# A Strassen–Winograd feed-forward kernel: two groups' second-matrix tiles kept for the first unit, its operands begun one group sooner, transposes moved to other gaps, and weight sums reordered

## The chip, the cores and the metric

The kernel runs on one core of one Trainium2 chip. The metric is the device time of one execution in microseconds (us). The tensor engine (PE) ran at a granted clock of 1.00 of full speed in every stretch looked at, so no difference here is one of clock.

## What is computed

The reference chains three blocks over a batch of 2 and a sequence of 768:

```python
x = attention(q, k, v)        # 8 heads of 64; a band of 31 keys beside block maxima of keys, block means of values
u = x + (relu(xt @ w_tok1) @ w_tok2).T          # over the sequence
x = u + relu(u @ w_ch1) @ w_ch2                 # 512 -> 1536 -> 512
xn = (x - mean) / sqrt(var + 1e-6) * g_ln
out = x + relu(xn @ w_ch1b) @ w_ch2b            # 512 -> 2048 -> 512
```

Float32 results are made of pairs of reduced-precision numbers, a high and a low part, so each product is three matmuls (high by high, high by low, low by high; lines L316, L317, L318).

## The kernel before, in words

Attention and the token mixing fill the first 95 us. From about 95 to 308 us stands the 512 to 1536 block, a loop over groups `(s, f, g)`: `g3` makes one first product (`g_('u', g)_f`, 12 matmuls 128x384) in a PSUM bank of the pool `ps_mm`; ScalarE (ACT, L700) makes the high part `ah` of its relu and VectorE (DVE, L701) the low part `al`; `g4` then makes three tiles of the second product (`acc`, three matmuls 128x512 each). Tiles of one group run between the first products of the next ones.

From 308 us on stands the last block as sixteen *units*. Units 0 to 7 (`unit`, for half the sequence) and 8 to 15 (`unit1`, the other half) each make seven Strassen–Winograd products `m`, of six matmuls 128x384. What a product leaves in its bank is taken up by adds into the running sums: `sm` by a copy of product 0 on ACT (L848), then `um`, `sm`, `wm`, `sm`, `wm` and `um`, `um` on DVE (L836), for products 1 to 6. Two of them read product 5. Behind the adds the relu parts are made (L827 on ACT, L828 on DVE). Between the products stand tiles `acc_x` of the unit before, which wait in the queue `pending`: `flow` issues ceil(pending / products left) of them behind product k, and then calls `step(k)`. In a unit of 2 to 7 twelve tiles wait, two behind each of the first five products, one behind each of the last two.

Three things are woven into that:

- **Transposes.** `prep_x(s)` makes the operands of the Strassen products from the normalized activations: eight times ACT normalizes (L623), PE transposes (`tx`, L656, three 128x128), ACT copies it out with a scale (L660), and ACT and DVE split it into parts (L641, L642) and sum operands (L671 to L683). `prep_x(0)`, for units 0 to 7, runs in the last groups of the block before. `prep_x(1)`, for units 8 to 15, starts in unit 1 and has two transposes in each of units 2 to 5.
- **Weight sums.** `w2_sums(p)`, p = 0 to 7, makes combinations of the second matrix for units 8 to 15: two adds `wx` (L787), three into `wt` (L796 to L799), two casts `wk` on ACT (L805), two subtractions on DVE (L809), two stores (L810, `w2t<-wk`, on SP's queue). For p of 2 and more, `wx` reads the second matrix of unit p where the unit itself reads it: two slots hold it, loaded in halves (L763, `slot<-w2s`). For p = 0 and 1 the matrix is read a second time (`read_again`, L773). The `wk` tiles live in the pool `spill`, with two buffers, so a cast waits until the store of two tiles earlier has landed.
- **Weight decoding** (`convert_all`), which ends in unit 1.

`ps_mm` has two banks, and products and transposes share them. So what comes behind a transpose needs the bank of the product ahead of the transpose, and waits until its adds have read it. On PE the order is the one in which the code issues (`manual_schedule`). On the other engines a scheduler orders the instructions by their readiness and priority; once built, the order is fixed, and an instruction that waits holds up those behind it on its engine. All loads and stores of this stretch are issued by SP.

Of the kernel before, what the change touches and what calls it, by code (L numbers as in the profile page):

```python
# [15 lines left out]
ALU = mybir.AluOpType  # L16
# [23 lines left out]
NP = F2 // 2  # L40
# [25 lines left out]
def f32(ap):  # L66
    return ap.bitcast(F32)


class Kern:  # L70
# [705 lines left out]
    def w2_sums(self, p):  # L776
        nc = self.nc
        tt = nc.vector.tensor_tensor
        new = lambda k: self.long(f"{k}{p}")
        if p < 2:  # L780
            src = self.again.pop(p)
        else:
            w = f32(self.w2_at(p))
            src = [w[:, 512 * i : 512 * i + 512] for i in range(4)]
        x = new("wx")
        for f in range(2):
            tt(x[:, 512 * f : 512 * f + 512], src[2 * f], src[2 * f + 1], op=ALU.add)  # L787
            if f:
                self.read.add(p)
                if p == 0:  # L790
                    self.read_again(1)
            yield
        t = new("wt")
        b = x.rearrange("p (f j n) -> p f j n", f=2, j=2)
        k = t.rearrange("p (k n) -> p k n", k=4)
        tt(k[:, 0:2], b[:, :, 1], b[:, 0], op=ALU.subtract)  # L796
        yield
        tt(k[:, 2], k[:, 0], b[:, 1, 1], op=ALU.subtract)
        tt(k[:, 3], k[:, 2], b[:, 1, 0], op=ALU.add)  # L799
        yield  # L800
        out = []
        for e in range(2):
            w = self.spill.tile([P, 1024], F32R, tag="sp", name=f"wk{e}_{p}")
            v = self.blocks(w)
            nc.scalar.copy(v[:, :, 0], k[:, 2 * e : 2 * e + 2])  # L805
            out.append((w, v))
        yield
        for e, (w, v) in enumerate(out):
            tt(v[:, :, 1], k[:, 2 * e : 2 * e + 2], f32(v[:, :, 0]), op=ALU.subtract)  # L809
            nc.sync.dma_start(self.w2t[p][:, 2 * e : 2 * e + 2].rearrange("p k t n -> p (k t n)"), f32(w))  # L810
            if e == 0:
                yield
        self.summed.add(p)
        yield
# [16 lines left out]
    def unit(self, n, pending, step):  # L831

        nc = self.nc
        s, p = divmod(n, NP)
        new = lambda k: self.tmp.tile([P, GN], F32, tag=k, bufs=1, name=f"{k}m_{n}")
        add = lambda o, x, y: nc.vector.tensor_tensor(o, x, y, op=ALU.add)  # L836
        bank = lambda k: self.ps_mm.tile([P, 512], F32, tag="mm", name=f"m{k}_{n}")
        a = {}
        for k in range(7):
            q = bank(k)  # L840
            self.product(7 * n + k, s, k, q)
            self.load_w1(7 * n + k + RING)
            q = q[:, :GN]
            urgent = ExitStack()
            urgent.enter_context(self.tc.high_priority(URGENT))
            if k == 0:
                s1 = new("s")
                nc.scalar.copy(s1, q)  # L848
            elif k == 1:
                u = new("u")  # L850
                add(u, q, s1)
            elif k == 2:
                add(s1, q, s1)
                a["C11"] = self.relu(f"{n}_11", s1)
            elif k == 3:
                w = new("w")
                add(w, q, u)
            elif k == 4:
                c = new("s")
                add(c, q, w)  # L860
                a["C12"] = self.relu(f"{n}_12", c)
            elif k == 5:
                add(w, q, w)
                a["C22"] = self.relu(f"{n}_22", w)
                add(u, q, u)
            else:
                add(u, q, u)
                a["C21"] = self.relu(f"{n}_21", u)
            urgent.close()
            self.flow(n, k, pending, step)  # L870
        self.load_w2(n + 1)
        out = []
        for name in ("C11", "C12", "C22", "C21"):
            f, i = int(name[1]) - 1, int(name[2]) - 1
            for j in range(GT):
                out.append((name, j, lambda f=f, i=i, j=j, x=a[name]: self.second(n, f, i, j, x)))
        return deque(x[2] for x in out)
# [256 lines left out]
    def run(self):  # L1134
        tc, nc, ctx = self.tc, self.nc, self.ctx
# [56 lines left out]
        first = self.small.tile([P, 1], F32, tag="first", name="first")  # L1192
# [16 lines left out]
        y = self.g2(1)  # L1209
        self.bg += [None] + [y] * ST  # L1210
        units = []
# [13 lines left out]
        later, pending = deque(), deque()  # L1225
        for n, (s, f, g) in enumerate(units):
# [10 lines left out]
                self.bg += [self.transpose_u(g + 2)] * CC  # L1237
            if f == 2 and s == 1:
                self.bg += [self.norm_stats(g - 2)] * (GT + 1)
            if (s, f, g) == (1, 5, 3):  # L1240
                later += [self.prep_x(0)] * 9
            elif later:
                self.bg.append(later.popleft())
            if prev is not None:
                while 2 * prev[1] + 1 not in self.half:
                    self.convert_all(4)
                blocks = self.g4(*prev)
                if n == len(units) - 1:
                    pending += blocks
                else:  # L1250
                    for fn in blocks:
                        fn()
                if prev[0] == ("u", 3) and prev[1] == 11:
                    for k in range(9):
                        self.load_w1(k)
                    self.load_w2(0)
# [29 lines left out]
        order.enter_context(tc.manual_schedule(engines={E.PE}))  # L1286
        pending += self.g4(*prev)
        self.summed, self.read, self.kp, self.again = set(), set(), {}, {}
        sums = (x for p in (2, 3, 4, 5, 0, 6, 1, 7) for x in self.w2_sums(p))
        pending.popleft()()  # L1290
        for n in range(2 * NP):

            def step(k):
                if n == 0 and k == 6:
                    for r in range(9, RING):
                        self.load_w1(r)
                self.convert_all(((2, 2, 2, 2, 2, 1, 0) if n == 0 else (3, 2, 2, 3, 2, 0, 2))[k])
                if (n, k) == (4, 0):
                    self.read_again(0)
                if n == 1 or n in range(2, 6) and k in (1, 5):  # L1300
                    for _ in range(2 if n == 1 and k in (1, 4) else 1):
                        self.start(1)
                        self.finish()

                if n > 2 or n == 2 and k > 5:
                    for _ in range((2, 0, 1, 2, 2, 0, 2)[k] if n < 6 else 2 if n == 7 or k in (0, 4) else 1):
                        next(sums, None)

            if n == 1:
                self.bg += [self.norm_stats(2)] * (GT + 1) + [self.norm_stats(3)] * (GT + 1)  # L1310
                self.bg += [self.prep_x(1)] * 9
            pending = (self.unit1 if n >= NP else self.unit)(n, pending, step)
# [89 lines left out]
```

## Time and profile before

| | us |
|---|---|
| device time, median of 3 runs (lowest, highest) | 569.76 (568.62, 571.74) |
| the profiled execution: its own time | 570.52 |
| the profiled execution: first to last instruction (span) | 568.5 |
| PE busy | 557.3 (98%) |
| VectorE busy | 404.7 (71%) |
| ScalarE busy | 274.8 (48%) |

The profile is of one execution, with times counted from its first instruction. A matmul's row gives its start, and an end that is modelled: the next matmul starts well before it. So a stall on PE is read from the distance between two starts, against the usual distance. A row of the timeline has start, duration, engine, line, operation, and what it writes and reads. A bracket gives the idle time of the engine ahead of it, and what ended that.

### The profile page before, as it was taken

The page shows a single profiled execution, that of the slowest core. Times are in us where ns is not written, and L with a number is a line of the kernel's source. Part 1 is how long each engine was busy: PE and PEld are TensorE (multiplying, and loading weights), DVE is VectorE, ACT ScalarE, POOL GpSimd, SP SyncE. Part 2 cuts the span into 40 slices and gives each one's busy share as a digit, 9 for nine tenths or more (in the row PEclk, how much of TensorE's full clock was granted, in tenths as well). Part 3 has the DMA queues.
Part 4 walks back from the last instruction along what each step waited for, and adds up shares of the span by engine and source line. Part 5 has one row for each costly group of instructions (what it writes and reads, how often), then busy time and mean ns, then how long its engine had stood idle before and what let it go on. Part 6 is the DMA issues. An engine that isn't in the chain of part 4 may idle for free.

```text
span 568.5 us, 10249 instructions
## 1 busy us (share of the span) xinstructions
PE 557.3 (98%) x3685; PEld 496.1 (87%) x3685; DVE 404.7 (71%) x977; ACT 274.8 (48%) x608; POOL 18.7 (3%) x41
## 2 busy tenths in 40 slices
PE   9999999999999999999999999999999999999997
PEld 4777779899998889889888898888898999999997
DVE  4998773647867887655568975768886876677771
ACT  4997673237755554544787234354333223333320
POOL 0011620000000000000000000000000000000000
PEclk9999999999999999999999999999999999999999
DMA  9969810425788878879757996787888998777545
GB/s 284 324 196 297 266 72 1 148 92 188 241 282 286 293 266 280 310 265 324 246 186 224 300 319 180 239 261 232 285 293 266 325 309 267 233 230 236 172 147 187
DMA packets 63655, 135.75 MB, mean 239 GB/s; under 512 B 5747, under 2 KB 22899, under 8 KB 63606
## 3 DMA queue, kind: packets, MB, share of 16 engines
q1 hardware_dynamic: 63600, 135.09, 72.1%
q8 instruction: 29, 0.48, 0.4%
q14 instruction: 20, 0.16, 0.1%
q10 hardware_dynamic: 6, 0.02, 0.0%
HBM read 100.49 MB, written 34.60 MB: 238 GB/s over the span
## 4 chain that ended last, share of the span: by engine, by line
PE 76%; DVE 7%; DMA 7%; ACT 6%; issue 2%; POOL 1%; ACTq 0%; POOLq 0%; DVEq 0%
PE m L316 7%; PE m L318 6%; PE m L317 6%; PE acc_x L318 3%; PE acc_x L317 3%; PE acc_x L316 3%; DMA slot<-w2s 2%; PE acc_y L318 2%; PE g L533 2%; PE acc_y L317 2%; PE acc_y L316 2%; ACT pr L477 2%; DMA w1s<-sps 1%; PE warm_ps L1132 1%; DMA stage<-in_wts_dram 1%
## 5 line engine op out<-in xcount | busy, mean ns | idle before, releaser
L316 PE MATMUL m<-slot,slot 128*128 128x384 f32 (+1 forms) x141 | 47.5, 337 | 1.1 <-DVE um L836 0.9
L318 PE MATMUL m<-slot,slot 128*128 128x384 f32 (+1 forms) x141 | 46.9, 332 | 0.0
L317 PE MATMUL m<-slot,slot 128*128 128x384 f32 (+1 forms) x141 | 46.8, 332 | 0.0
L318 PE MATMUL acc_x<-slot,al 128*128 128x512 f32 x96 | 37.8, 394 | 0.0
L317 PE MATMUL acc_x<-slot,ah 128*128 128x512 f32 x96 | 37.8, 394 | 0.0
L316 PE MATMUL acc_x<-slot,ah 128*128 128x512 f32 x96 | 37.5, 391 | 0.0
L477 ACT ACTIVATE pr<-sn,mn 128x120 f32<-128x120 f32 x96 | 29.9, 386 | 4.8 <-DVE mn L462 4.7
L316 PEld LDWEIGHTS m<-slot,slot 128*128 128x128 f32 x141 | 26.5, 188 | 4.2 <-DVE um L836 1.9
L317 PEld LDWEIGHTS m<-slot,slot 128*128 128x128 f32 x141 | 26.5, 188 | 1.6
L318 PEld LDWEIGHTS m<-slot,slot 128*128 128x128 f32 x141 | 26.5, 188 | 0.0
L827 ACT ACTIVATE ah<-sm 128x384 fp32r<-128x384 f32 x16 | 8.4, 524 | 36.7 <-DVE sm L836 36.7
L141 ACT ACTIVATE dec<-stage 128x512 f32<-128x512 f32 x36 | 24.4, 677 | 2.4 <-DMA stage<-in_wts_dram 2.4
L164 DVE SCALAR_TENSOR_TENSOR dec<-stage,dec 128x512 uint32<-128x512 uint32 x36 | 24.8, 688 | 0.9
L462 DVE CUSTOM_DVE_ANT_0 sn<-scores,mask 128x120 f32<-128x120 f32 x96 | 21.2, 277 | 5.4 <-PE scores L443 5.3
L533 PE MATMUL g<-u,tok 128*128 128x256 f32 x96 | 21.6, 381 | 0.0
L318 PEld LDWEIGHTS acc_x<-slot,al 128*128 128x128 f32 x96 | 18.0, 188 | 4.0
L168 DVE SCALAR_TENSOR_TENSOR dec<-stage,dec 128x512 uint32<-128x512 uint32 x23 | 15.9, 690 | 7.3 <-ACT stage L141 7.3
L318 PE MATMUL acc_y<-slot,al_s 128*128 128x256 f32 x72 | 20.1, 280 | 0.0
L533 PEld LDWEIGHTS g<-u,tok 128*128 128x128 f32 x96 | 17.9, 190 | 2.5 <-issue 0.2
L317 PE MATMUL acc_y<-slot,ah_s 128*128 128x256 f32 x72 | 20.1, 279 | 0.0
L623 ACT ACTIVATE xn<-u,nb,rs 128x128 f32<-128x128 f32 x48 | 20.1, 484 | 0.0
L316 PE MATMUL acc_y<-slot,ah_s 128*128 128x256 f32 x72 | 20.0, 278 | 0.0
(1493 smaller groups left out, 1707.1 us busy)
## 6 DMA issues: line engine op xcount, KB each, us to landing
stage<-in_wts_dram SPq DMA_DIRECT2D x62, 512.0 KB, 4.5
slot<-w1s SPq DMA_DIRECT2D x94, 256.0 KB, 3.7
w1s<-sps SPq DMA_DIRECT2D x16, 512.0 KB, 3.6
w2s<-sp SPq DMA_DIRECT2D x16, 512.0 KB, 3.9
slot<-w2s SPq DMA_DIRECT2D x16, 512.0 KB, 5.0
w2t<-wk SPq DMA_DIRECT2D x16, 512.0 KB, 4.6
slot<-w2t SPq DMA_DIRECT2D x8, 768.0 KB, 5.0
slot<-w2s SPq DMA_DIRECT2D x22, 256.0 KB, 4.4
```

The lines of the kernel that those rows point to most:

```text
L141: fold = lambda out: nc.scalar.activation(out, high, AF.Prelu, scale=2.0**-112, alpha=-(2.0**32))
L164: put(m, t[:, :, 0], 29, m, op0=ALU.logical_shift_right, op1=ALU.bitwise_or)
L168: put(m, t[:, :, 1], 3, m, op0=ALU.logical_shift_left, op1=ALU.bitwise_or)
L316: nc.tensor.matmul(out, lhs[0], rhs[0], start=first, stop=False)
L317: nc.tensor.matmul(out, lhs[0], rhs[1], start=False, stop=False)
L318: nc.tensor.matmul(out, lhs[1], rhs[0], start=False, stop=last)
L462: nc.vector.tensor_tensor_reduce(sn[:, u], ps[:, u % 2, u // 2, :NK], self.mask[:, mv], scale=-SCALE, scalar=3e38, op0=ALU.add, op1=ALU.mi ...
L477: self.nc.scalar.activation(self.pr[n][:, u], sn[:, u], AF.Exp, bias=mn[:, u : u + 1], scale=-1.0)
L533: nc.tensor.matmul(ps[:, :256], self.tok1(st, t), self.u[:, b * ST + st, 256 * hf : 256 * hf + 256], start=st == 0, stop=st == ST - 1,)
L623: nc.scalar.activation(xn[:, j], self.u[:, g * GT + j, cc * P : cc * P + P], AF.Identity, bias=nb[:, j : j + 1], scale=rs[:, j : j + 1],)
L827: nc.scalar.activation(ah, x, AF.Relu)
L1132: self.nc.tensor.matmul(self.wps, self.warm[:, :P], self.warm, start=True, stop=True)
```

## The change

The change has four parts. The tiles `acc` of the last two groups of the 512 to 1536 block join `pending`, not those of the last alone; two of them are issued ahead of unit 0, not one. `prep_x(0)` is put into the loop at group (1, 8, 2), not (1, 5, 3). The transposes of `prep_x(1)` in units 2 to 5 stand behind products 1 and 3 (counted from 0), not 1 and 5. The weight sums of p = 2 to 7 and those of p = 0 and 1 run as two sequences, with new places in the units, `read_again(0)` moves from unit 4 to unit 2, and each `wx` add is issued behind the add `um`, `sm` or `wm` that the code issued last.

```diff
@@ w2_sums
         for f in range(2):
-            tt(x[:, 512 * f : 512 * f + 512], src[2 * f], src[2 * f + 1], op=ALU.add)
+            with self.tc.issue_after(self.reader.ins):
+                tt(x[:, 512 * f : 512 * f + 512], src[2 * f], src[2 * f + 1], op=ALU.add)
@@ unit
-        add = lambda o, x, y: nc.vector.tensor_tensor(o, x, y, op=ALU.add)
+        def add(o, x, y):
+            self.reader = nc.vector.tensor_tensor(o, x, y, op=ALU.add)
+
@@ run
-            if (s, f, g) == (1, 5, 3):
+            if (s, f, g) == (1, 8, 2):
                 later += [self.prep_x(0)] * 9
...
-                if n == len(units) - 1:
+                if n >= len(units) - 2:
                     pending += blocks
...
-        sums = (x for p in (2, 3, 4, 5, 0, 6, 1, 7) for x in self.w2_sums(p))
-        pending.popleft()()
+        sums = (x for p in range(2, NP) for x in self.w2_sums(p))
+        first = (x for p in range(2) for x in self.w2_sums(p))
+        for _ in range(2):
+            pending.popleft()()
...
-                if (n, k) == (4, 0):
+                if (n, k) == (2, 0):
                     self.read_again(0)
-                if n == 1 or n in range(2, 6) and k in (1, 5):
+                if n == 1 or n in range(2, 6) and k in (1, 3):
...
-                if n > 2 or n == 2 and k > 5:
-                    for _ in range((2, 0, 1, 2, 2, 0, 2)[k] if n < 6 else 2 if n == 7 or k in (0, 4) else 1):
+                if n > 1:
+                    for _ in range((0, 0, 1, 1, 2, 1, 2)[k]):
                         next(sums, None)
+                if 2 < n < 7 and k < 2:
+                    for _ in range(1 if (n, k) in ((3, 0), (5, 1)) else 2):
+                        next(first, None)
```

On PE the first transpose of `prep_x(0)` moves ahead of the product `g_('u', 3)_9`. The difference there (+ is a row of the changed kernel):

```order
 L316 MATMUL acc_('u', 3)_0_2841<-slot_1544,ah_('u', 3)_8_3211 128x512
 L317 MATMUL acc_('u', 3)_0_2841<-slot_1544,ah_('u', 3)_8_3211 128x512
 L318 MATMUL acc_('u', 3)_0_2841<-slot_1544,al_('u', 3)_8_3212 128x512
+L656 MATMUL tx_0_3263<-ident,xn_0_3218 128x128 x3
 L316 MATMUL acc_('u', 3)_1_2842<-slot_1544,ah_('u', 3)_8_3211 128x512
 L317 MATMUL acc_('u', 3)_1_2842<-slot_1544,ah_('u', 3)_8_3211 128x512
```

So `g_('u', 3)_9`, which comes six matmuls later, has a transpose between itself and the product `g_('u', 2)_12`, where before it had none.

On PE at the end of unit 0, before (`m5_0` is product 5 of unit 0, `m0_1` product 0 of unit 1; the rows between repeat these):

```order
L318 MATMUL m5_0_3760<-slot6_1542,slot8_1544 128x384
L316 MATMUL m6_0_3774<-slot9_1545 128x384
...
L318 MATMUL m6_0_3774<-slot9_1545 128x384
L316 MATMUL m0_1_3792<-slot3_104,extra_1744 128x384
L317 MATMUL m0_1_3792<-slot3_104,extra_1744 128x384
```

and in the changed kernel:

```order
L318 MATMUL m5_0_3752<-slot6_1542,slot8_1544 128x384
L316 MATMUL acc_('u', 3)_1_2842<-slot2_103,ah_('u', 3)_14_3625 128x512
...
L316 MATMUL m6_0_3770<-slot9_1545 128x384
...
L316 MATMUL acc_('u', 3)_2_2843<-slot2_103,ah_('u', 3)_14_3625 128x512
...
L316 MATMUL m0_1_3792<-slot3_104,extra_1744 128x384
```

Three products stood back to back, and now a tile of three matmuls stands between each two.

On DVE in unit 2 and the start of unit 3, before (`wm_2<-m3_2` is the add that reads product 3 of unit 2, `wx3` the weight sum of unit 3's matrix in `slot11`):

```order
L836 TENSOR_TENSOR wm_2_4051<-m3_2_4043,um_2_4004 128x384
L787 TENSOR_TENSOR wx3_4246<-slot11_1737 128x512
L836 TENSOR_TENSOR sm_2_4067<-m4_2_4059,wm_2_4051 128x384
...
L828 SCALAR_TENSOR_TENSOR al_2_21_4118<-um_2_4004,ah_2_21_4117 128x384
L787 TENSOR_TENSOR wx3_4246<-slot11_1737 128x512
L836 TENSOR_TENSOR um_3_4157<-m1_3_4149,sm_3_4137 128x384
```

and the same two adds in the changed kernel, in unit 3:

```order
L838 TENSOR_TENSOR sm_3_4157<-m2_3_4212,sm_3_4157 128x384
L788 TENSOR_TENSOR wx3_4231<-slot11_1737 128x512
...
L838 TENSOR_TENSOR wm_3_4241<-m3_3_4233,um_3_4175 128x384
L678 TENSOR_TENSOR t1_0_T2_4198<-t1_0_T3_4197,f1_0_B11_4024 128x384
L788 TENSOR_TENSOR wx3_4231<-slot11_1737 128x512
L797 TENSOR_TENSOR wt3_4288<-wx3_4231 128x512
L838 TENSOR_TENSOR sm_3_4276<-m4_3_4268,wm_3_4241 128x384
```

The first `wx3` add moved from product 4 of unit 2 to behind product 2 of unit 3, the second from product 1 of unit 3 to behind product 3. (The lines of the changed kernel lie one to three higher: L788 is L787 of before, L838 is L836.)

## Rows read from the trace of the kernel before

**Rows 1.** The page, busy time and share of each engine:

```profile
PE 557.3 (98%) x3685; PEld 496.1 (87%) x3685; DVE 404.7 (71%) x977; ACT 274.8 (48%) x608; POOL 18.7 (3%) x41
```

**Rows 2.** Stretches of units 2 to 6: from:to, length, busy time by engine, clock, DMA:

```profile
335.68:353.44 17.76, 16.61 (x85) 14.73 (x84) 10.78 (x25) 7.28 (x17) 0.00 (x0) 1.00 0.70 226
353.44:370.72 17.28, 16.82 (x85) 14.74 (x84) 11.49 (x23) 7.86 (x18) 0.00 (x0) 1.00 0.72 228
370.72:387.82 17.10, 16.64 (x85) 14.76 (x84) 13.01 (x26) 8.53 (x20) 0.00 (x0) 1.00 0.74 231
387.82:404.54 16.72, 16.63 (x86) 14.74 (x85) 14.82 (x30) 8.70 (x19) 0.00 (x0) 1.00 0.88 283
404.54:420.26 15.72, 15.72 (x79) 14.18 (x78) 13.66 (x28) 3.92 (x8) 0.00 (x0) 1.00 0.85 286
```

**Rows 3.** The timeline of DVE, then of PE, in units 2 and 3:

```profile
348.31 0.69 DVE L787 TENSOR_TENSOR wx<-slot 128x512 f32<-128x512 f32 x1 [3.16 <-DMA slot<-w2s]
...
351.00 0.55 DVE L836 TENSOR_TENSOR um<-m,um 128x384 f32<-128x384 f32 x1
...
351.61 0.45 PE L316 MATMUL m<-slot,extra 128*128 128x384 f32 x1 [1.15 <-DVE um L836]
...
358.32 0.49 PE L656 MATMUL tx<-ident,xn 128*128 128x128 f32 x3
358.76 0.44 PE L316 MATMUL m<-slot,slot 128*128 128x384 f32 x1
```

**Rows 4.** Line L763: who waited for it, and time from issue to landing:

```profile
  DVE wx L787: 12.2, 8
...
DMA to landing us min/median/max: 3.6/5.0/6.0
```

**Rows 5.** The timeline of PE at both ends of unit 0:

```profile
307.38 0.40 PE L318 MATMUL acc_('u', 3)_0_2841<-slot,al_('u', 3)_13_3585 128*128 128x512 f32 x1
308.08 0.45 PE L316 MATMUL m<-slot 128*128 128x384 f32 x1 [0.30 <-DVE al_('u', 3)_14_3635 L701]
...
318.86 0.33 PE L317 MATMUL m<-slot 128*128 128x384 f32 x1
319.03 0.34 PE L318 MATMUL m<-slot 128*128 128x384 f32 x1
319.91 0.44 PE L316 MATMUL m<-slot,extra 128*128 128x384 f32 x1 [0.54 <-DVE um L836]
```

**Rows 6.** The timeline of ACT, DVE and PE around the product `g_('u', 3)_9`:

```profile
270.61 0.62 ACT L227 CAST sp<-dec 128x512 fp32r<-128x512 f32 x1 [2.63 <-DMA w2s<-sp]
...
273.01 0.55 DVE L701 SCALAR_TENSOR_TENSOR al_('u', 2)_12_3253<-g_('u', 2)_12_3239,ah_('u', 2)_12_3252 128x384 fp32r<-128x384 f32 x1
...
272.10 0.33 PE L316 MATMUL g_('u', 3)_9_3286<-xt,slot 128*128 128x384 f32 x1
...
274.90 0.49 PE L656 MATMUL tx<-ident,xn 128*128 128x128 f32 x3
275.15 0.48 PE L316 MATMUL acc_('u', 2)_1_2659<-slot,ah_('u', 2)_12_3252 128*128 128x512 f32 x1
275.46 0.40 PE L317 MATMUL acc_('u', 2)_1_2659<-slot,ah_('u', 2)_12_3252 128*128 128x512 f32 x1
...
276.17 0.39 PE L317 MATMUL acc_('u', 2)_2_2660<-slot,ah_('u', 2)_12_3252 128*128 128x512 f32 x1
276.39 0.40 PE L318 MATMUL acc_('u', 2)_2_2660<-slot,al_('u', 2)_12_3253 128*128 128x512 f32 x1
277.31 0.45 PE L316 MATMUL g_('u', 2)_13_3326<-xt,slot 128*128 128x384 f32 x1 [0.53 <-DVE al_('u', 3)_9_3300 L701]
277.60 0.34 PE L317 MATMUL g_('u', 2)_13_3326<-xt,slot 128*128 128x384 f32 x1
```

**Rows 7.** Line L810: who waited for it, and time from issue to landing:

```profile
  ACT wk L805: 2.1, 1
DMA to landing us min/median/max: 3.0/4.6/6.7
```

## The prediction

> **What bounds the kernel now.** I read the page first. PE is busy for 98% of the span [rows 1], so nothing but an emptier PE makes this kernel shorter: the change removes no matmul, and all that it can give is the time in which PE stood. Next I read the stretches of the units it touches. A unit of 2 to 6 holds seven products and twelve tiles; those of 2 to 5 hold two transposes as well. Unit 6, with weight sums but no transposes, takes 15.72 us; units 2 to 5 take 17.76, 17.28, 17.10 and 16.72 [rows 2]. A transpose set costs 0.25 us to the next start, and that next matmul takes 0.31 to its successor where a tile's matmul usually takes 0.22 to 0.23: 0.33 us in all [rows 6]. So a unit with two of them, and no stall, takes 15.72 + 0.66 = 16.38. What goes beyond that is stall: 1.38, 0.90, 0.72 and 0.34, together **3.34 us**.
>
> Who causes it is in the timeline. In unit 2 DVE stands 3.16 us behind the add `wx`, until a load of the second matrix has landed at 348.3; the adds that free the product banks queue up behind it, and product 6 starts at 351.61, right behind the add `um` of 351.00 [rows 3]. Over the kernel the `wx` adds stood 12.2 us for such loads, eight times [rows 4]. That is one cause. The other is the place of the second transpose: behind product 5 stand one tile (0.69) and the transposes (0.33), then product 6, which needs product 5's bank, and that bank is read by two adds of 0.55. They have 1.0 us where they need 1.0 to 1.2 with both hand-overs (an add that ends at 351.55 lets the product start at 351.61 [rows 3]).
>
> Outside the units I read single bubbles, as distances between starts. A product's matmul usually starts 0.17 behind the one before (318.86 to 319.03), a tile's 0.23. Product 0 of unit 0 comes 0.70 behind a tile's last matmul, 0.47 too late; product 0 of unit 1, at 319.91, comes 0.88 behind the last matmul of product 6, 0.71 too late [rows 5]. After each such wait the first matmul takes 0.29 instead of 0.17, 0.12 more (277.31 to 277.60 [rows 6]). So these two cost 0.59 and 0.83. `g_('u', 2)_13` starts 0.92 behind a tile: 0.69 + 0.12 = 0.81 lost, to `al_('u', 3)_9` [rows 6].
>
> **The change part by part.**
>
> *Nine waiting tiles in unit 0, not six.* One tile now stands behind every product of unit 0. Before, products 5 and 6 of unit 0 and product 0 of unit 1 stood back to back, and the last of them waited for the second add of product 5, with one product (1.05) to cover it. Two tiles come between, 1.38, twice the wait of 0.71. Two tiles instead of one stand between `g_('u', 3)_14` and unit 0: 0.69 more for an `al` that was 0.47 late. I take both: **+0.59 and +0.83**. Bounds: 0 (if DVE is as late as PE is) and 1.42. The matmuls are the same ones; the accumulator adds of these tiles come later on DVE, around the start of unit 1, and the first tile of unit 1 that needs one of those accumulators stands behind two products and three tiles, over 4 us on.
>
> *Operands one group sooner.* The first transpose now stands ahead of `g_('u', 3)_9`, whose bank is then that of `g_('u', 2)_12`, freed by `al_('u', 2)_12`. That one ran from 273.01 to 273.56, late because ACT stood 2.63 us behind a cast that waited for a store until 270.61; nothing in the change moves that store. The product started at 272.10; with 0.33 of transposes ahead it could start at 272.43, and must wait until 273.62: 1.19 + 0.12 = 1.31 lost [rows 6]. In exchange the wait of 0.81 at `g_('u', 2)_13` goes, since PE reaches it 1.6 us later and its `al` (ending at 277.26) is not much later than before. The transposes that follow have the same distances as before. Net **−0.50**; between +0.81 (no new wait) and −1.31 (the old wait stays). I take the sum because each of its parts has a row.
>
> *Transposes behind products 1 and 3.* Behind product 3 stand two tiles (1.38) and the transposes (0.33), and one add has to be done: 0.55 in 1.71. *Sums timed by loads.* A `wx` add now follows the add of product 2 or 3 of the unit whose matrix it reads. The second half of that matrix is loaded as the unit starts and lands 3.6 to 6.0 us later [rows 4]; in two units (3 and 7) two stores now stand ahead of it on SP, which I estimate to cost up to 2 us: 8.0 at worst. The add behind product 3 comes at 7.6 + 1.05 + 0.6 = 9.2 us with one transpose ahead (7.6 is three products of 1.05, six tiles of 0.69 and the transposes), 8.9 without. So DVE no longer stands there, and none of the stalls of units 2 to 5 has its cause left: **+3.34**, between 1.5 (only the late adds of product 5 mended) and 3.34.
>
> *A new wait in unit 4.* There the cast `wk` of p = 0 comes onto ACT right after the stores of p = 3 were issued, and with two `spill` buffers it waits for the first of them to land. Such a wait stands in the trace once, 2.1 us, and a store takes 3.0 to 6.7 us, 4.6 in the median [rows 7]. Behind the cast on DVE queue the subtraction of p = 0 and, behind it, the add `sm` of product 2, for which product 3 waits. Issue 0.6 to 1.5 us into the unit (an estimate: one or two operations of 0.55 to 0.69 behind the last `um` of unit 3), landing 4.6, then cast, subtraction and add, about 0.6 + 0.7 + 0.6: product 3 could start between 7.1 and 8.0, where its turn is at 7.6. From 0 to 0.4, and 2.5 with the longest landing. I take **−0.3**, the middle of the upper part, since SP's queue is busy there. In unit 6 the same pair comes ahead of product 4, whose turn is over 2 us later, so nothing.
>
> The re-read of p = 0 and 1 stands earlier in SP's queue; the loads of first-matrix tiles behind it are issued twelve products (over 25 us) ahead, so a few microseconds there are covered.
>
> Sum: 0.59 + 0.83 − 0.50 + 3.34 − 0.3 = **4.0 us** of the profiled execution's 570.52 (span 568.5 and 2.0 around it), giving 566.6. That execution stands 0.76 above the median of the three runs, 569.76; taken off the median: **565.8 us**.
>
> A rule that speaks against the moved transposes: the Trainium skill ("Perfetto Trace Analysis", section "Matmuls") wants independent matmul groups to rotate through different banks, so that one is read out while the next is filled. Here the rotation has two banks, and a transpose takes one of them wherever it stands. By that rule the wait would move with the transpose, not go. The trace agrees for one of the places kept: the product behind the transposes of 358.32 came 0.44 behind them, 0.19 above 0.25, and with the slow matmul some 0.23 was lost, but DVE had stood behind `wx` just before [rows 3].
>
> **The rivals.**
>
> *Waits at every transpose.* If all eight transposes of units 2 to 5 keep such a 0.23, 1.8 of the 3.34 stay: gain 2.2, **567.6**. For it: two banks. Against: units 4 and 5, whose stalls are 0.72 and 0.34 in all with one transpose behind product 1 and one behind 5.
>
> *No new wait.* If the first transpose finds its bank free and unit 4's store lands early, the gain is 0.59 + 0.83 + 0.81 + 3.34 = 5.6: **564.2**. For it: ACT's order there changes, with a normalization moved ahead of the cast. Against: that cast waits for a store, not for ACT.
>
> *The sums stay late (the change does not do what it says).* If DVE has its sums ahead of the urgent adds again, in other places, only unit 0 gains: 1.42 − 0.50 = 0.9: **568.9**. Against: the built order, where each `wx` follows an add.
>
> *Slower.* The second-half load of every unit from 2 to 7 comes so late that the `wx` behind product 3 stands 3.16 us, as in unit 2 now, which cost 1.38 there. Six units lose 8.3 us against 3.34 now; with 0.9 − 0.3 from the rest, 4.4 us slower: **574.1**. It decides only if a load lands over 12 us after its unit's start, where rows show 3.6 to 6.0 after issue: SP would have to stand 6 us in each unit.
>
> **How the numbers follow.** The measurement of this kernel can tell about 0.5%, 2.85 us, from no change; the bound is 566.9. Chances: forecast 0.50, waits at every transpose 0.18, no new wait 0.14, sums late 0.13, slower 0.05. The range from 564.0 to 568.0 leaves out slower, sums late and a little below. Faster by over 0.5%: 0.14, most of the forecast's 0.50 and a part of the second: 0.62. Within: 0.33. Slower: 0.05.
>
> **What would show it.** Units 2 to 5 of 16.4 us each; unit 4 up to 0.4 longer, with product 3 behind `sm`. `g_('u', 3)_9` starting about 1.2 us late behind `al_('u', 2)_12`, and no wait at `g_('u', 2)_13`. Unit 0 without gaps of more than 0.1. No idle time of DVE behind `slot<-w2s` in units 2 to 7. Wrong I am if DVE stands behind another thing ahead of an add, most likely a `wk` subtraction whose cast waits for a store, or if a stall of the same size appears at product 4 behind the moved transposes.

## The result, and the profile after

The changed kernel takes 565.56 us in the median of six runs (563.0 to 567.01), where the kernel before took 570.37 in six runs: ratio 0.9907, 95% interval 0.9885 to 0.9930. That is 5.3 us by the ratio, 4.0 to 6.6 by the interval, and 4.8 between the medians. The forecast was 565.8 and 4.0. Of all runs timed for this document one, of the kernel with the sums as before (572.34 us), was in the slower state and is left out of its median below.

The profiled execution took 565.9 us, with a span of 563.8. The busy row of its page:

```profile
PE 555.5 (99%) x3685; PEld 496.4 (88%) x3685; DVE 404.6 (72%) x977; ACT 275.7 (49%) x608; POOL 18.6 (3%) x41
```

PE does the same 3685 matmuls in a shorter span. The stretches of units 0 to 6 (from:to, length, then busy time by engine), which answer to [rows 2]:

```profile
306.71:319.01 12.30, 12.30 (x64) 11.30 (x63) 11.55 (x26) 5.72 (x13) 0.00 (x0) 1.00 0.79 264
319.01:334.68 15.67, 15.67 (x79) 14.14 (x78) 11.80 (x31) 3.91 (x9) 0.00 (x0) 1.00 0.98 336
334.68:351.03 16.35, 16.35 (x85) 14.68 (x84) 10.27 (x24) 8.42 (x19) 0.00 (x0) 1.00 0.66 209
351.03:367.38 16.35, 16.35 (x85) 14.70 (x84) 14.71 (x31) 8.35 (x20) 0.00 (x0) 1.00 0.81 273
367.38:383.73 16.35, 16.35 (x85) 14.70 (x84) 12.79 (x25) 9.35 (x21) 0.00 (x0) 1.00 0.90 306
383.73:400.10 16.37, 16.37 (x86) 14.71 (x84) 15.22 (x31) 7.72 (x18) 0.00 (x0) 1.00 0.77 241
400.10:415.82 15.72, 15.72 (x79) 14.18 (x78) 11.91 (x23) 5.16 (x10) 0.00 (x0) 1.00 0.95 306
```

In every row the length is PE's busy time: PE stands nowhere between 306.7 and 415.8. Units 2 to 5 took 68.86 us before and take 65.42 now: 3.44 saved, where 3.34 were forecast. `wx` (L788 now) never waits for a load; the row that named 12.2 us in [rows 4] is gone from the view of the loads, L763.

A single execution must be read with care here. Up to the product `g_('u', 2)_12` PE and DVE run the same instructions in both kernels (on ACT one normalization comes sooner), and the changed one came there at 269.20, the one before at 267.91. So the change is better measured from that product's start to the start of unit 8: 168.04 us before (267.91 to 435.95), 162.31 now (269.20 to 431.51), **5.7 us** saved. That is the rival "no new wait" (5.6), not the forecast (4.0). The interval of the clock holds both values; only the traces can tell them apart. The experiments begin with that difference.

### The profile page after: what moved, and what is told of

The parts are those of the page before. It is cut to its first block, busy times and chain, and to the rows that moved or that the text cites. A ratio compares the mean times of both kernels' runs of the same rounds, so it can differ in the third digit from the quotient of the medians.

```text
span 563.8 us, 10255 instructions
## 1 busy us (share of the span) xinstructions
PE 555.5 (99%) x3685; PEld 496.4 (88%) x3685; DVE 404.6 (72%) x977; ACT 275.7 (49%) x608; POOL 18.6 (3%) x41
## 4 chain that ended last, share of the span: by engine, by line
PE 81%; DMA 6%; ACT 6%; DVE 5%; issue 1%; POOL 1%; ACTq 0%; SPq 0%; POOLq 0%
PE m L316 7%; PE m L318 7%; PE m L317 7%; PE acc_x L317 4%; PE acc_x L318 4%; PE acc_x L316 4%; DMA stage<-in_wts_dram 4%; PE acc_y L318 2%; PE acc_y L317 2%; PE acc_y L316 2%; PE g L533 2%; ACT pr L477 2%; PE warm_ps L1135 2%; PE scores L443 1%; PE pt L486 1%; PE av L505 1%
## 5 line engine op out<-in xcount | busy, mean ns | idle before, releaser
L317 PEld LDWEIGHTS acc_x<-slot,ah 128*128 128x128 f32 x96 | 18.0, 187 | 1.9
```

Source lines behind the costliest of these rows:

```text
L317: nc.tensor.matmul(out, lhs[0], rhs[1], start=False, stop=False)
```

## The experiments

The table gives, for each kernel, the median of its runs, the ratio to the kernel before on the same chip, the length from the start of `g_('u', 2)_12` to unit 8 (*stretch*), and that of units 2 to 5, both from the profiled execution. The kernel before was profiled once.

| kernel | median us (runs) | ratio, 95% interval | stretch | units 2 to 5 |
|---|---|---|---|---|
| before | 570.37 (6) | | 168.04 | 68.86 |
| changed | 565.56 (6) | 0.9907, 0.9885 to 0.9930 | 162.31 | 65.42 |
| changed, second execution | 565.67 (4) | 0.9912, 0.9884 to 0.9939 | 163.90 | 65.41 |
| changed, third execution | 564.93 (6) | 0.9903, 0.9872 to 0.9933 | 163.78 | 66.20 |
| sums as before | 567.22 (9) | 0.9942, 0.9914 to 0.9970 | 164.90 | 67.98 |
| transposes as before | 568.59 (10) | 0.9954, 0.9922 to 0.9986 | 164.48 | 67.43 |
| sums and transposes as before | 567.77 (10) | 0.9968, 0.9939 to 0.9996 | 165.69 | 68.01 |
| sums without the tie | 568.02 (7) | 0.9940, 0.9914 to 0.9967 | 163.26 | 66.08 |
| waiting tiles as before | 567.29 (10) | 0.9943, 0.9911 to 0.9974 | 163.33 | 65.42 |
| start of the operands as before | 567.18 (6) | 0.9950, 0.9922 to 0.9978 | 165.35 | 65.51 |
| tiles and start as before | 566.74 (5) | 0.9926, 0.9900 to 0.9951 | 165.22 | 66.36 |
| first transpose moved on | 564.85 (4) | 0.9878, 0.9843 to 0.9914 | 161.98 | 65.43 |
| the same again | 566.12 (6) | 0.9920, 0.9893 to 0.9946 | 161.96 | 65.41 |
| the same, subtractions tied | 564.53 (6) | 0.9902, 0.9871 to 0.9933 | 162.33 | 65.77 |

The runs of one kernel spread over 0.8 to 7.5 us, so the medians do not decide between theories that lie 1 us apart: six of the twelve medians of the experiments lie outside the times that their theories gave, by up to 0.7 us (those with the transposes, the tiles, sums and transposes, or tiles and start as before, the third execution, and the repeat with the moved transpose). Nor is the profiled execution always a middle one. With the transposes and with the waiting tiles as before it was the fastest of ten (564.71 against a median of 568.59, 564.41 against 567.29), and without the tie the second fastest of seven (566.11 against 568.02). What the traces of these three show as lost may be less than most executions lose.

**The changed kernel again.** No edit.

> The changed kernel again, for a second profiled execution. In the first one PE came to the product g_('u', 3)_9 1.3 us later than in the kernel before, by delays in code that the change does not touch, and found its bank free, where I had forecast 1.31 us lost. Theory A (chance): that wait depends on when PE arrives; where PE arrives without the 1.3 us, g_('u', 3)_9 again stands behind al_('u', 2)_12, up to 1.2 us. Theory B (gone for good): ScalarE and VectorE follow PE, and there is no wait whenever PE arrives. Both: units 2 to 5 take 16.3 to 16.5 us each, as in the first execution (16.35, 16.35, 16.35, 16.37). Time 563 to 567 us.

Theory A. PE came to `g_('u', 2)_12` at 267.44 this time, 1.8 us sooner than in the first execution, and `g_('u', 3)_9` stood. Its row here, and the cast on ACT (L227) that waits for the store, first of the first execution, then of this one:

```profile
270.37 0.62 ACT L227 CAST sp<-dec 128x512 fp32r<-128x512 f32 x1 [0.31 <-DMA w2s<-sp]
```

```profile
270.44 0.62 ACT L227 CAST sp<-dec 128x512 fp32r<-128x512 f32 x1 [1.88 <-DMA w2s<-sp]
...
273.42 0.45 PE L316 MATMUL g_('u', 3)_9_3298<-xt,slot 128*128 128x384 f32 x1 [1.29 <-DVE al_('u', 2)_12_3257 L701]
```

The store let the cast go at 270.4 in both; only PE was earlier. The distance from the tile's last matmul ahead of it is 1.46 us too long, and 0.11 on the next matmul: 1.57, where 1.31 were forecast.

**A third execution**, with more rounds.

> The changed kernel, a third profiled execution and more rounds. By the theory of the store: g_('u', 3)_9 waits when the store w2s<-sp of 266 us lands later than 1.5 us behind the start of g_('u', 2)_12's last third, that is, the loss is (landing of the store + 3.0) minus (start of g_('u', 2)_12 + 4.5), where that is positive: -0.4 in the first execution (none seen) and 1.4 in the second (1.46 seen). Units 2 to 5 16.35 each. Time 565 to 566 us.

No wait at `g_('u', 3)_9`, though PE came to `g_('u', 2)_12` at 267.48, as early as in the second execution. This time it was the store that differed. Its issue on SP and the cast, first of the second execution, then of this one:

```profile
265.58 0.32 SPq L262 DMA_DIRECT2D w2s<-sp  x1
...
270.44 0.62 ACT L227 CAST sp<-dec 128x512 fp32r<-128x512 f32 x1 [1.88 <-DMA w2s<-sp]
```

```profile
264.96 0.32 SPq L262 DMA_DIRECT2D w2s<-sp  x1
...
268.23 0.61 ACT L227 CAST sp<-dec 128x512 fp32r<-128x512 f32 x1
```

The store was issued 0.6 us sooner and held the cast until 4.9 us after its issue there, and here not beyond 3.3. The cast went at 268.23 without standing, so `al_('u', 2)_12` was done early. But two others show, in unit 1 and in unit 4, where I had put 0.3 us (timeline of PE, ACT and DVE):

```profile
327.59 0.44 PE L316 MATMUL m<-slot,slot 128*128 128x384 f32 x1 [0.43 <-DVE sm L838]
...
374.67 0.44 PE L316 MATMUL m<-slot,extra 128*128 128x384 f32 x1 [0.52 <-DVE sm L838]
...
372.81 0.62 ACT L806 CAST wk<-wt 128x512 fp32r<-128x512 f32 x1 [4.62 <-DMA w2t<-wk]
...
373.46 0.69 DVE L810 TENSOR_TENSOR wk<-wt,wk 128x512 fp32r<-128x512 f32 x1 [2.80 <-ACT wk L806]
374.07 0.55 DVE L838 TENSOR_TENSOR sm<-m,sm 128x384 f32<-128x384 f32 x1
```

The last four rows are one chain: the cast of p = 0 stands 4.62 us for a store, the subtraction on DVE 2.80 us for the cast, the add `sm` comes behind it, and product 3 of unit 4 behind that, 0.68 late and 0.11 on the next (unit 4: 17.14). In the first execution the same cast stood 3.30 us, until 372.53, and unit 4 had begun 1.0 us later: no loss. The wait in unit 1 (0.59 + 0.11) is of the same kind: `sm` stood behind a decoding subtraction whose cast waited 4.89 us for a store, and behind statistics of the normalization (1.25 us) that came between. The prediction did not list it.

**The weight sums as before** (order, steps, place of the re-read, no tie; one hunk of the edit is shown):

```diff
-        sums = (x for p in range(2, NP) for x in self.w2_sums(p))
-        first = (x for p in range(2) for x in self.w2_sums(p))
+        sums = (x for p in (2, 3, 4, 5, 0, 6, 1, 7) for x in self.w2_sums(p))
```

> The changed kernel with the weight sums of before (order 2, 3, 4, 5, 0, 6, 1, 7, the steps of before, read_again(0) in unit 4, wx adds free to go where the scheduler puts them); transposes stay behind products 1 and 3. Theory A (two causes, loads and place): VectorE stands behind slot<-w2s again, 10 to 12 us in all, and PE stalls where a wait of VectorE is longer than the cover: units 2 and 3 together 1.0 to 2.0 us longer than 16.4 each, units 4 and 5 near 16.4. Rival B (the place alone): with two tiles and a transpose ahead of every bank that one add frees, all four units stay at 16.4. Rival C (the sums alone): all of the 3.3 us comes back. Time 565.5 + 1.0 to 2.0 by A, 565.5 by B, 569 by C.

The stretches of units 2 to 5:

```profile
334.18:350.57 16.39, 16.39 (x86) 14.73 (x86) 11.20 (x26) 7.63 (x19) 0.00 (x0) 1.00 0.68 210
350.57:366.92 16.35, 16.35 (x86) 14.70 (x85) 12.12 (x25) 8.94 (x20) 0.00 (x0) 1.00 0.73 234
366.92:385.01 18.09, 16.61 (x85) 14.73 (x84) 12.25 (x24) 7.79 (x17) 0.00 (x0) 1.00 0.71 224
385.01:402.16 17.15, 16.63 (x85) 14.74 (x84) 14.18 (x30) 8.82 (x20) 0.00 (x0) 1.00 0.80 261
```

The waits of DVE from 300 to 440 us (total, times, longest), and DVE and PE in unit 4, show the cause:

```profile
DVE wx L787 <- DMA slot<-w2s: 13.9, 9, 2.4
```

```profile
372.56 0.69 DVE L787 TENSOR_TENSOR wx<-slot 128x512 f32<-128x512 f32 x1 [1.76 <-DMA slot<-w2s]
373.17 0.55 DVE L837 TENSOR_TENSOR um<-m,sm 128x384 f32<-128x384 f32 x1
...
373.78 0.44 PE L316 MATMUL m<-slot,slot 128*128 128x384 f32 x1 [1.48 <-DVE um L837]
```

DVE stands behind loads again, 13.9 us in nine waits. Units 2 and 3, which I expected to lose, lose nothing; units 4 and 5 lose 1.7 and 0.8, 2.56 in all. Kind as in theory A, place and size not: most of the waits fall where no product needs the next add soon; in units 4 and 5 a `wx` stands right ahead of the add `um` of product 1, and product 2, behind the transposes, waits for that.

**The transposes as before.**

```diff
-                if n == 1 or n in range(2, 6) and k in (1, 3):
+                if n == 1 or n in range(2, 6) and k in (1, 5):
```

> The changed kernel with the transposes of units 2 to 5 behind products 1 and 5 again; the weight sums stay as changed. Theory A (two causes): product 6 of units 2 to 5 comes behind the two adds of product 5 with 1.02 us of cover, 0.1 to 0.65 us late in each unit: 0.26 to 0.63 as in units 3 to 5 of before, 1.2 to 2.2 us in all, and VectorE does not stand behind loads. Rival C (the sums alone): no stall, 16.4 us each. Time 567 to 568 by A, 565.5 by C.

The same stretches:

```profile
331.61:348.32 16.71, 16.61 (x86) 14.73 (x84) 10.24 (x25) 7.47 (x18) 0.00 (x0) 1.00 0.66 205
348.32:365.04 16.72, 16.62 (x86) 14.75 (x85) 13.91 (x28) 7.62 (x18) 0.00 (x0) 1.00 0.84 268
365.04:382.32 17.28, 16.63 (x85) 14.75 (x84) 14.02 (x29) 9.85 (x23) 0.00 (x0) 1.00 0.88 289
382.32:399.04 16.72, 16.63 (x86) 14.75 (x85) 14.48 (x29) 7.48 (x17) 0.00 (x0) 1.00 0.74 236
```

Theory A: 2.01 us, with no wait of DVE for loads. Three units lose 0.37, the price of the place alone: 0.26 that the second add of product 5 overshoots the 1.02 us of cover, and 0.11 on the next matmul. Unit 4 loses 0.93. There a cast `wk` stood 4.00 us for a store, until 371.90; from 372.55, where the subtraction behind it starts, DVE has no gap until past the second add of product 5 (379.86 to 380.41), which comes that much later.

```profile
371.90 0.62 ACT L806 CAST wk<-wt 128x512 fp32r<-128x512 f32 x1 [4.00 <-DMA w2t<-wk]
...
379.86 0.55 DVE L838 TENSOR_TENSOR um<-m,um 128x384 f32<-128x384 f32 x1
...
380.45 0.44 PE L316 MATMUL m<-slot,slot 128*128 128x384 f32 x1 [0.65 <-DVE um L838]
```

**Both as before** (the two edits above together).

> The changed kernel with both the weight sums and the transposes of units 2 to 5 as before: the first two parts of the change alone. Undone one by one, the sums cost 2.5 us in units 2 to 5 and the transposes 2.0, where the kernel before lost 3.3 there. Theory A (both waits end at the same adds, so they overlap): 3.0 to 3.8 us of stall in units 2 to 5, less than 4.5, and no gap in unit 0. Rival (they add up): 4.5. Time 568.5 to 569.5 us by A, 570 by the rival.

Units 2 to 5 lose 2.59 us, and unit 7 another 0.77 (a `wx` wait ahead of a product there). Singly the two cost 2.56 and 2.01. So they do not add up, but the reason that theory A gave, one and the same add held twice, does not come out of the units. Lost in units 2 to 5, one by one: 0.04, 0, 1.74 and 0.78 with the sums as before, 0.36, 0.37, 0.93 and 0.35 with the transposes, 1.15, 0.54, 0.37 and 0.53 with both. In unit 2 the two together cost more than their sum: with the late place a load wait of 1.79 us reaches product 6, and with the early place one of 2.25 does not. In unit 4 they cost less than either, because the `wx` that held product 2 there with the sums alone (1.76 us) waits only 0.71 in this execution, and the store's wait of the new sums is not there. The 3.0 to 3.8 us of theory A come out only with unit 7. Of the 3.36 that units 2 to 5 and 7 lose here, the moved transposes alone save 0.80 and the new sums alone 1.35; both together save all of it.

**The new sums without the tie.**

```diff
-            with self.tc.issue_after(self.reader.ins):
-                tt(x[:, 512 * f : 512 * f + 512], src[2 * f], src[2 * f + 1], op=ALU.add)
+            tt(x[:, 512 * f : 512 * f + 512], src[2 * f], src[2 * f + 1], op=ALU.add)
```

> The changed kernel without the tie of each wx add to the add that the code issued last; order and steps of the sums as changed. The built order then has wx adds of units 3 and 4 ahead of adds of the unit before again. Theory A: the tie is what keeps VectorE from standing behind loads: VectorE stands 5 to 12 us behind slot<-w2s, and units 2 to 5 lose 1 to 3 us. Rival: the new steps and the separate sums of p = 0 and 1 do it, and units 2 to 5 stay within 0.3 us of 16.35. Time 566.5 to 568.5 by A, 565.5 by the rival.

DVE stands 9.8 us behind loads, as theory A has it, but PE loses only 0.66 us in units 2 to 5, 0.50 of it in unit 2. The longest of the waits, in unit 5, costs nothing:

```profile
396.24 0.69 DVE L787 TENSOR_TENSOR wx<-slot 128x512 f32<-128x512 f32 x1 [2.15 <-DMA slot<-w2s]
396.85 0.55 DVE L837 TENSOR_TENSOR sm<-m,wm 128x384 f32<-128x384 f32 x1
...
398.66 0.34 PE L316 MATMUL m<-slot,slot 128*128 128x384 f32 x1
```

The add behind it is done at 397.40, over 1 us before product 6, the next user of that bank. A wait of 1.76 us, in the kernel with the sums as before, cost 1.74: what counts is how soon the add behind it is needed. Neither theory's range holds the 0.66; the median of 568.02 lies in theory A's range of times. So the traces leave open what the tie is worth.

**The waiting tiles as before.**

```diff
-                if n >= len(units) - 2:
+                if n == len(units) - 1:
...
-        for _ in range(2):
-            pending.popleft()()
+        pending.popleft()()
```

> The changed kernel with the tiles of one group alone kept for unit 0 (six waiting tiles, one issued ahead of unit 0, as before); the operands still begin one group sooner. Theory A: the gaps at both ends of unit 0 come back: 0.4 to 0.6 us at product 0 of unit 0 and 0.7 to 0.9 at product 0 of unit 1, 1.0 to 1.5 in all; units 2 to 5 stay at 16.35. Rival: with the operands ready sooner DVE has less to do there, and neither gap comes back. Time 566.5 to 567 us by A, 565.5 by the rival.

The one wait of PE that came back, in the timeline:

```profile
317.44 0.44 PE L316 MATMUL m<-slot,extra 128*128 128x384 f32 x1 [0.44 <-DVE um L838]
```

Half of theory A: 0.61 + 0.11 at product 0 of unit 1 are back, and there is no gap at product 0 of unit 0 (product 1 loses 0.20). The tiles cure the one. For the other this run is no test, since it has another order there. Its rows, then those of the changed kernel:

```profile
301.21 0.49 PE L656 MATMUL tx<-ident,xn 128*128 128x128 f32 x3
...
305.74 0.33 PE L316 MATMUL m<-slot 128*128 128x384 f32 x1
...
306.97 0.56 DVE L701 SCALAR_TENSOR_TENSOR al_('u', 3)_14_3651<-g_('u', 3)_14_3637,ah_('u', 3)_14_3650 128x384 fp32r<-128x384 f32 x1 [0.27 <-ACT ah_('u', 3)_14_3650 L700]
```

```profile
305.00 0.49 PE L656 MATMUL tx<-ident,xn 128*128 128x128 f32 x3
...
306.02 0.40 PE L316 MATMUL acc_('u', 3)_1_2842<-slot,ah_('u', 3)_12_3538 128*128 128x512 f32 x1
...
306.71 0.34 PE L316 MATMUL m<-slot 128*128 128x384 f32 x1
...
305.84 0.56 DVE L701 SCALAR_TENSOR_TENSOR al_('u', 3)_14_3626<-g_('u', 3)_14_3612,ah_('u', 3)_14_3625 128x384 fp32r<-128x384 f32 x1
```

With the tiles as before the last transpose stands ahead of `g_('u', 3)_14`, so product 0 takes the transposes' bank and starts 1.8 us before that `al` is done. In the changed kernel the transpose stands behind `g_('u', 3)_14`, and product 0 needs that product's bank. It is free at 306.40, and with one tile less the turn of product 0 would have been at 306.02 (an estimate from these rows). With neither the tiles nor the earlier operands the gap is there (0.47, in the kernel below with both as before).

**The start of the operands as before.**

```diff
-            if (s, f, g) == (1, 8, 2):
+            if (s, f, g) == (1, 5, 3):
```

> The changed kernel with prep_x(0) put into the loop at group (1, 5, 3) again, one group later; the nine waiting tiles stay. Theory A: the wait of g_('u', 2)_13 behind al_('u', 3)_9 comes back (0.81 in the kernel before), if PE arrives as early as there; the operand T4 of unit 0 is ready one group later, and its product 6 is the last, so unit 0 either is not held up or by under 1 us. Rival B: unit 0's products wait for their operands, several us, and that is why the start was moved. Time 565.5 to 566.5 by A, over 567 by B.

The waits of PE in its timeline:

```profile
278.09 0.44 PE L316 MATMUL g_('u', 2)_13_3326<-xt,slot 128*128 128x384 f32 x1 [0.59 <-DVE al_('u', 3)_9_3300 L701]
...
307.07 0.33 PE L656 MATMUL tx<-ident,xn 128*128 128x128 f32 x1 [0.27 <-ACT xn L623]
...
310.31 0.44 PE L316 MATMUL m<-slot,slot 128*128 128x384 f32 x1 [0.39 <-ACT slot L641]
311.30 0.44 PE L317 MATMUL m<-slot,slot 128*128 128x384 f32 x1 [0.54 <-DVE slot L642]
```

Both theories in part: the old wait is back (0.75 + 0.11), and unit 0 waits for its operands (0.43 for a normalization, 0.55 and 0.82 for splits). With two groups' tiles set aside the block before ends sooner, so the operands must begin sooner: those two parts of the change belong together. In the next kernel, with both as before, unit 0 does not wait for an operand.

**Tiles and start both as before** (the two edits above together).

> The changed kernel with the tiles kept and the start of prep_x(0) both as before: the weight sums and the transposes of units 2 to 5 alone. Theory A: the three stalls of before come back, 0.8 at g_('u', 2)_13, 0.6 and 0.8 at both ends of unit 0, 2.0 to 2.3 us, and units 2 to 5 stay at 16.35. Rival: undone singly, the tiles cost 0.7 and the start of the operands 2.9, so the two together cost 3.6. Time 567 to 568 us by A, 569 by the rival.

Theory A: 0.32, 0.47 and 0.70, each with 0.11, at `g_('u', 2)_13` and at both ends of unit 0: 1.8 us. Against the kernel before, the sums and the transposes alone save 2.5 in units 2 to 5; unit 4 lost 0.93 here by the chain of the third execution (its cast stood 4.79 us).

**The first transpose moved on.** One group sooner still, with none ahead of `g_('u', 3)_9`:

```diff
-            if (s, f, g) == (1, 8, 2):
-                later += [self.prep_x(0)] * 9
+            if (s, f, g) == (1, 4, 3):
+                prep = self.prep_x(0)
+                later += [prep, prep, None] + [prep] * 7
```

> The changed kernel with the first transpose of prep_x(0) one more group sooner, ahead of g_('u', 2)_12, and none ahead of g_('u', 3)_9; the other seven stay. Theory A (the wait of g_('u', 3)_9 is for the bank of g_('u', 2)_12, whose eviction stands behind a cast that waits for a store): g_('u', 3)_9 has a bank of its own and no wait, whenever the store lands; g_('u', 2)_12 waits for al_('u', 3)_8, which is done over 1 us ahead: no loss. The gain on the changed kernel is 0 to 1.6 us, by what each execution loses there. Rival: the wait moves to g_('u', 2)_12, or to g_('u', 2)_13, and is as long. Time 564.5 to 565.5 by A, 565.6 by the rival.

> The kernel with the first transpose one more group sooner and none ahead of g_('u', 3)_9, again, timed in more rounds beside the changed kernel on the same chip. Theory: g_('u', 3)_9 has no wait in this execution either; 0 to 1.6 us shorter than the changed kernel by what that one loses there, 0.7 in the middle: 564.5 to 565.5 us.

`g_('u', 3)_9` has no wait in either, and none moved elsewhere. PE and DVE in the first of the two:

```profile
273.24 0.33 PE L316 MATMUL g_('u', 3)_9_3298<-xt,slot 128*128 128x384 f32 x1
...
273.44 0.55 DVE L701 SCALAR_TENSOR_TENSOR al_('u', 2)_12_3269<-g_('u', 2)_12_3255,ah_('u', 2)_12_3268 128x384 fp32r<-128x384 f32 x1
```

In the first of the two the product starts 0.75 us *before* the `al` of the product ahead of it is done (273.44 + 0.55): in the changed kernel it would have stood there. The stretch is 161.98 and 161.96, against 162.31 to 163.90. By the clock the gain over the changed kernel is not resolved: 564.85 and 566.12 against 565.56, 565.67 and 564.93. On the one chip that ran both, the repeat had 566.12 and the changed kernel 564.93.

**The same, with the subtractions of p = 0 behind product 4 in unit 4** (the tie is set for those of every p):

```diff
+            with self.tc.issue_after(self.reader.ins):
-            tt(v[:, :, 1], k[:, 2 * e : 2 * e + 2], f32(v[:, :, 0]), op=ALU.subtract)
+                tt(v[:, :, 1], k[:, 2 * e : 2 * e + 2], f32(v[:, :, 0]), op=ALU.subtract)
...
-                if 2 < n < 7 and k < 2:
+                if 2 < n < 7 and k in ((0, 3) if n == 4 else (0, 1)):
```

> The kernel with the moved first transpose, and in unit 4 the two subtractions wk of p = 0 tied behind the add sm of product 4 (their casts stay where they were, and still wait for the stores of p = 3). In the third execution of the changed kernel product 3 of unit 4 came 0.68 us late behind the add sm, which stood behind such a subtraction whose cast had waited 4.6 us for a store. Theory A (the subtraction ahead of sm passes the store's wait on): the cast waits 3 to 5 us again, and product 3 of unit 4 is not late whenever the store lands; unit 4 takes 16.35. Rival: product 3 is late for the transpose's copy, which stands behind the same cast on ScalarE, and stays late by 0 to 0.9 us. What can go wrong: the stores of p = 0 start about 4 us later, and the cast of p = 4 at the end of unit 4 waits for them, with the copy sm of unit 5 behind it; that has about 2 us of cover. Time 564 to 566 us by both.

The cast in unit 4, a later one ahead of unit 5's first copy `sm`, and the stretches of units 4 and 5:

```profile
372.62 0.62 ACT L806 CAST wk<-wt 128x512 fp32r<-128x512 f32 x1 [4.73 <-DMA w2t<-wk]
...
385.11 0.62 ACT L806 CAST wk<-wt 128x512 fp32r<-128x512 f32 x1 [1.71 <-DMA w2t<-wk]
```

```profile
366.05:382.39 16.34, 16.34 (x85) 14.71 (x84) 10.89 (x21) 8.26 (x19) 0.00 (x0) 1.00 0.79 263
382.39:399.12 16.73, 16.64 (x85) 14.76 (x84) 16.36 (x34) 8.59 (x19) 0.00 (x0) 1.00 0.86 277
```

Theory A: the cast waits as long as in the third execution, 4.73 us, and starts as late in unit 4 (6.57 us after its start, 6.47 there), and unit 4 loses nothing. The transposes' copy still stands behind that cast on ACT, so the rival falls; it is one execution. The price is of the kind that was feared: in unit 5 a cast waits for a store until 385.11, `ah` and the copy `sm` stand behind it, and DVE, busy for 16.36 of 16.73 us of unit 5, comes to the add `um` of product 1 late. Product 2 starts 0.28 late, and with its slow first matmul 0.37 is lost there.

## Why the prediction was right, and where its terms were off

The kernel became faster by about the sum forecast, and for most of it by the mechanisms named. Three executions of it save 5.7, 4.1 and 4.3 us over the stretch against the one profiled execution of the kernel before, 4.7 in the mean, where 4.0 were forecast. That the time came within 0.3 us of the forecast is partly luck: the median of the kernel before was 0.6 lower in the three runs that the forecast started from than in all six, and two of its terms differ from one execution to the next, by up to 1.57 and 0.79. Term by term:

- *Ends of unit 0, 0.59 and 0.83.* Both gaps are gone in all three executions. That the tiles cure the second is shown by undoing them (0.72 lost). For the first, the rows of the changed kernel agree with the prediction, since the second tile covers the end of `al_('u', 3)_14`; undoing the tiles could not show it, because that moved the last transpose too.
- *Operands one group sooner, −0.50.* The chain was right, from store to cast to `al` to product; the term was taken as fixed, and it is not. The old wait of 0.81 is gone each time. The new wait, put at 1.31, was 0, 1.57 and 0 in three executions, so the term was +0.81, −0.76 and +0.81. The wait depends on two times that were taken as given. PE came to `g_('u', 2)_12` up to 3.2 us apart, after the same instructions (265.97 to 269.20 in the runs here): 1.3 us later than in the kernel before in the first execution, where the cast went at 270.37, nearly as before. And the store let the cast go by 268.23 in the third, 2.2 us sooner than in the second, with PE equally early. Nothing in the change moves that store, but that does not make it land at the same time.
- *Units 2 to 5, 3.34.* 3.44 measured in the first execution. That both causes count, the load and the place behind product 5, is shown by undoing each (2.56 and 2.01). That the two do not add up was not foreseen. The two adds of product 5 need 1.28 us by the loss with 1.02 of cover, a little over the 1.0 to 1.2 reckoned.
- *Unit 4, −0.3.* The chain is there each time, with the cast standing 3.3 to 4.8 us, and product 3 lost 0, 0 and 0.79 in three executions (0.93 with tiles and start as before). The bounds held; the mean of 0.26 is near the value taken, though no execution lost it. Tying the subtractions points to DVE's queue, not ACT's, as what passes the wait on.
- Not listed: the wait in unit 1 of the third execution, 0.70.

The rival "waits at every transpose" falls: with two banks, and a transpose in one of them, product 4, behind the moved transposes, starts on time in units 2 to 5 of all three executions. The rule of the Trainium skill ("Perfetto Trace Analysis", section "Matmuls"), that independent groups rotate through different banks so that one is read out while the next is filled, is not against that: it does not say how long the readout may take. What decides here is the cover between the product and the next user of its bank: 1.71 us for one add is enough, 1.02 for two is not. "The sums stay late" and "slower" fell with the `wx` waits.

What stays open: what makes PE arrive early or late at `g_('u', 2)_12`, and why the store there lets its cast go at such different times. One part of the first is seen, a wait behind an `al` near 185 us, of 1.45 us in the first execution, 0.41 in the third and none in the second, but not what delayed that `al`. A third `spill` buffer would test both remaining waits, in units 1 and 4, from the other side; it was not tried.

## What to carry to other kernels

With few banks, count for each bank what stands between the product that fills it and the next user, and how many reads have to end in that time; move a short user (a transpose) to the gap whose product has one reader. An instruction that waits for a transfer should not stand in an in-order queue right ahead of an add that frees a bank soon needed: place it by when its data land, and look for the same chain through a second engine and a buffer pool. Two delays in one stretch can cost less together than singly, or more (both were seen here, in different units): price and test them singly and together, and unit by unit. Profile a kernel more than once before a wait on a transfer is called there or gone.

## What was not expected of the hardware

Stores of 512 KB took from 3.0 to 6.7 us to land in the kernel before [rows 7], and 3.5 to 5.5 in the changed one, and a wait that ends on one was there in one execution and gone in the next, in the same program. Such a wait ends when the store has landed, so PE's delay or lead upstream can be taken up in it: in the first two executions of the changed kernel PE was 1.8 us apart at `g_('u', 2)_12` and 0.17 us apart at unit 8 (431.51 and 431.34). The third came as early as the second, and lost its lead at the two other waits of this kind (unit 8 at 431.26). With the first transpose moved on no such wait reached PE, and a lead of 1.7 us (267.39 against 269.07) was still there at unit 8 (429.35 against 431.05).
